# Routed attention and a SoLU layer in one program: cluster products in one pass, u centred in place of w_out, and a new instruction order

## The chip, the core and the metric

The program runs on one core of one Trainium2 chip. The metric is the time of one execution in microseconds (us) of device time. The kernel before takes 224.29 us, the median of three runs (224.18 to 224.49).

The core has five engines, and each works through its own list of instructions in order: TensorE (PE in the profile; its weight loads are PEld), VectorE (DVE), ScalarE (ACT), GpSimd (POOL) and SyncE (SP, which here only issues transfers). They meet at semaphores.

## The reference

```python
q_n = q / (norm(q) + 1e-6)          # k and the centroids c alike
q_assign = argmax(q_n @ c_n.T)      # 16 clusters for each head
k_assign = argmax(k_n @ c_n.T)
mask   = q_assign[:, :, :, None] == k_assign[:, :, None, :]
scores = where(mask, q @ k.T / 8, -1e9)
attn   = softmax(scores)
x      = (attn @ v)                 # 4 batches x 768 tokens, 8 heads x 64 -> 3072 x 512
h      = x @ w_in                   # 512 -> 1024
solu   = h * softmax(h)
ln     = (solu - mean(solu)) / sqrt(var(solu) + 1e-6) * g_ln
out    = ln @ w_out                 # 1024 -> 512
```

There are 4 batches, 8 heads, 768 tokens and a head size of 64. Inputs and output are float32.

## The kernel before, in words

**Attention.** The work goes by batch and by pair of heads: 16 pairs. For each pair q and k are brought to a layout with the head's 64 values on the partitions (`xt`). In the first batch TensorE turns them over; in the other three VectorE does (`xt`, line 444). The pair's products with the centroids (`clusters`, `cl` in the order) are float32 matmuls into `csc`. VectorE then turns `csc` back (`tb`), takes the maximum over the 16 clusters (`mx`), compares (`oh`, the one-hot) and turns the one-hot again (`ot`). The one-hot rows are placed (`pl`) under the bfloat16 copies of q and k (`ca`) in the tile `qk`, so that one matmul of 80 or 96 rows gives score plus bias, and a pair of tokens of different clusters gets a score that the exponential sends to nothing. `bl` blanks the rows that the second head of a pair must not see. Scores (`S`, 294 banks of up to 512 columns) are exponentiated on ScalarE (`E`, line 635), multiplied with v and a column of ones (`V`, 192 blocks of 128 tokens, line 654), and divided by the sums on VectorE (`N`, lines 666 and 679) into `x`.

In the first batch tokens lie so that the pairs 1 to 3 have two tokens in each column of the turned tile (`twelve` in the code is true for them). Their cluster products run in two passes that add up in PSUM, one for each head of the pair, with weights (`c_by_two`) that are zero outside that head's rows: 8 matmuls of 384 columns for a pair (line 484), where a later pair has 4 (line 489).

**The layer.** The 3072 tokens go in 24 blocks f of 128. For each: x is turned (`tx`, a transposing transfer, or TensorE for the first and last), h is made (`h`, 4 parts of two matmuls of 512 columns, line 744), its maximum taken (`hm`, line 750), exponentiated (`ex`, line 756), multiplied (`u` = e * h, line 763), u is turned (`tu`, a transposing transfer, line 768; TensorE and a copy for the last two blocks, lines 732 to 740), the output product runs (`y`, 4 parts, line 813), and the result is scaled by `alpha` (`sc`, lines 830 and 832) and stored (`ou`). The statistics of u (`bn`, `ag`, lines 774 and 778) give `alpha` on GpSimd (`at`, `al`, lines 784 to 793).

The mean of u over the 1024 features must be taken away. The kernel before does it in the weights: with w_g = w_out times g_ln, the mean of w_g over its 1024 rows is taken from each row, and then u needs no centring. That is `su` (8 instructions on VectorE, lines 595 and 598), `me` (TensorE, line 604) and `ce` (8 instructions on VectorE, line 607), once for the program.

**What sets the order.** A class `Weave` holds for each engine a text such as `S2 tp S2 cl S3`: kinds of work in the order in which they stand, where the next of that kind is taken. A second table (`AWAY`) says which pieces run on another engine than their usual one. In a planning pass at build time the class walks through the texts and emits the instructions. The costs given to `add` are used for this plan alone. On the chip an engine does what stands next in its list as soon as what it needs is there, and nothing behind it passes it.

`UNITS`, `BANKS` and `FIRST` (line 279) set in which order the scores of the first batch come: pair 1 with its first and second third of queries, then pairs 2 and 3 alike, and the last thirds of all at the end.

## Time and profile before

| | |
|---|---|
| median of 3 runs | 224.29 us (224.18 to 224.49) |
| span of the profiled execution, first to last instruction | 222.4 us |
| median less span | 1.9 us |
| mean granted TensorE clock | 0.999 |
| matmul work on TensorE, share of the span | 214.8 us, 97% |
| VectorE | 199.1 us, 90% |
| ScalarE | 194.7 us, 88% |
| GpSimd | 126.6 us, 57% |
| first score matmul | 9.90 us |
| first h matmul in the chain of waits | 45.30 us |
| first y matmul | 56.73 us |
| last y matmul ends | 219.03 us |

The page of the profile gives busy time by engine, the chain of waits that ended last (followed back from the last instruction: each step is either work or what it waited for), the costliest groups of instructions with a mean duration, and the transfers. A busy time is the union of an engine's instructions. Matmuls overlap one another in the pipeline, so a busy TensorE can still be standing behind a wait; the chain of waits shows better where it stood.

### The profile page before, as it was taken

How to read it: one execution, taken by the hardware profiler on the slowest of the kernel's cores; microseconds unless marked ns; L12 is line 12 of the kernel's file. 1: busy time of each engine (PE TensorE's matmuls, PEld its weight loads, DVE VectorE, ACT ScalarE, POOL GpSimd, SP SyncE). 2: the span in 40 equal slices, each digit the busy share in tenths (PEclk: the TensorE clock that was granted, in tenths of full speed). 3: DMA queues.
4: the chain of work that ended last, by engine and by line, in shares of the span. 5: the costliest groups of instructions: out<-in, count | busy, mean ns of one | idle time of the engine just before them, and what ended most of it. 6: DMA issues, size and time to landing. Idle time of an engine off the chain costs nothing.

```text
span 222.4 us, 6852 instructions
## 1 busy us (share of the span) xinstructions
PE 214.8 (97%) x2518; PEld 151.8 (68%) x2548; DVE 199.1 (90%) x363; ACT 194.7 (88%) x382; POOL 126.6 (57%) x252
## 2 busy tenths in 40 slices
PE   8999899999999999999999999999999999999993
PEld 7765577767777687777777666676767767665452
DVE  2789999999999999899989999999999979999891
ACT  3899999999999999999999989999999989795352
POOL 3189597759884986188837674783746101226131
PEclk9999999999999999999999999999999999999999
DMA  6998989797799979899999897998922928565623
GB/s 157 352 388 221 193 165 284 203 172 165 127 175 237 180 141 215 136 193 166 153 211 239 156 185 150 151 168 158 230 99 50 115 78 145 117 165 121 166 98 143
DMA packets 122433, 38.74 MB, mean 174 GB/s; under 512 B 111448, under 2 KB 117152, under 8 KB 122400
## 3 DMA queue, kind: packets, MB, share of 16 engines
q1 hardware_dynamic: 121680, 37.82, 79.8%
q10 hardware_dynamic: 720, 0.49, 0.7%
q8 instruction: 20, 0.33, 0.7%
q14 instruction: 13, 0.11, 0.1%
HBM read 23.11 MB, written 6.29 MB: 132 GB/s over the span
## 4 chain that ended last, share of the span: by engine, by line
PE 91%; DVE 3%; issue 2%; ACT 2%; DVEq 0%; ACTq 0%
PE sps L627 27%; PE hreg L744 18%; PE yps L813 17%; PE ops L654 16%; PE csc L489 4%; PE hreg L627 2%; PE idle_p L859 2%; PE csc L484 1%; PE hreg L403 1%; PE hreg L396 1%; ACT qk L468 1%; PE hreg L813 1%; ACT e L635 1%; DVE u L763 1%; DVE w_sum L598 1%
## 5 line engine op out<-in xcount | busy, mean ns | idle before, releaser
L635 ACT ACTIVATE e<-sps 128x512 bf16<-128x512 f32 (+1 forms) x276 | 143.2, 609 | 10.2 <-PE sps L627 9.8
L627 PE MATMUL sps<-qk 96*128 96x256 bf16 (+5 forms) x600 | 87.4, 263 | 0.7 <-ACT e L635 0.4
L627 PEld LDWEIGHTS <-qk 96*128 96x128 bf16 (+1 forms) x636 | 59.6, 121 | 24.5 <-issue 8.8
L654 PEld LDWEIGHTS <-e 128*128 128x128 bf16 x1152 | 49.9, 97 | 9.3 <-issue 1.9
L654 PE MATMUL ops<-v,e 128*128 128x65 bf16 x1152 | 54.3, 193 | 0.4 <-DVE x L679 0.4
L744 PE MATMUL hreg<-w_in_sb,xT 128*128 128x512 bf16 x177 | 48.3, 378 | 0.8
L813 PE MATMUL yps<-w_out_c,uT 128*128 128x512 bf16 x169 | 45.1, 379 | 0.8
L540 POOL COPY qk<-oht 32x384 f32<-32x384 f32 (+1 forms) x49 | 24.2, 494 | 21.5 <-DVE oht L521 15.7
L763 DVE TENSOR_TENSOR u<-e_sb,hreg 128x1024 bf16<-128x1024 bf16 (+1 forms) x25 | 29.1, 1169 | 2.7 <-ACT e_sb L756 2.1
L774 DVE BATCH_NORM_STATS2 bs<-u 128x6 f32<-128x512 bf16 x48 | 31.3, 677 | 0.0
L750 DVE TENSOR_REDUCE nmax<-hreg 128x1 f32<-128x1024 f32 x24 | 29.1, 1213 | 2.0 <-PE hreg L744 1.7
L756 ACT ACTIVATE e_sb<-hreg,nmax 128x1024 bf16<-128x1024 f32 x24 | 26.9, 1121 | 4.5 <-DVE nmax L750 4.4
L790 POOL TENSOR_SCALAR esq<-es,mv 128x1 f32<-128x1 f32 x24 | 8.3, 344 | 33.6 <-DVE mv L778 30.3
L813 PEld LDWEIGHTS <-uT 128*128 128x128 bf16 x200 | 18.0, 97 | 13.1 <-issue 0.3
L744 PEld LDWEIGHTS <-xT 128*128 128x128 bf16 x192 | 17.6, 97 | 11.3 <-ACT e L635 0.3
L472 POOL TENSOR_SCALAR qk<-xt 64x768 bf16<-64x768 f32 (+1 forms) x27 | 22.2, 823 | 3.5 <-DVE xt L444 1.7
L444 DVE STREAM_TRANSPOSE xt<-raw 128x768 f32<-128x768 f32 x24 | 22.2, 949 | 0.0
L470 POOL CAST qk<-xt 64x768 bf16<-64x768 f32 (+1 forms) x25 | 20.9, 836 | 1.2
L679 DVE TENSOR_TENSOR x<-ops,den 128x256 bf16<-128x256 f32 (+1 forms) x39 | 18.9, 486 | 1.3
L784 POOL TENSOR_SCALAR es<-esum 128x1 f32<-128x1 f32 x24 | 5.6, 236 | 20.9 <-ACT e_sb L756 20.4
L793 POOL TENSOR_TENSOR alpha<-esq,halves 128x1 f32<-128x1 f32 x24 | 13.8, 574 | 2.0
L830 ACT ACTIVATE y<-yps,alpha 128x512 f32<-128x512 f32 x15 | 10.4, 695 | 4.3 <-PE yps L813 3.0
(85 smaller groups left out, 206.9 us busy)
## 6 DMA issues: line engine op xcount, KB each, us to landing
vf<-in_v_dram SPq DMA_DIRECT2D x16, 384.0 KB, 4.6
out_dram<-y SPq DMA_DIRECT2D x23, 256.0 KB, 2.5
raw<-in_q_dram SPq DMA_DIRECT2D x50, 96.0 KB, 3.8
raw<-in_k_dram SPq DMA_DIRECT2D x50, 96.0 KB, 3.0
w_g<-in_moe_w_out_dram SPq DMA_DIRECT2D x4, 512.0 KB, 8.3
w_st<-in_moe_w_in_dram SPq DMA_DIRECT2D x4, 512.0 KB, 6.2
raw<-in_q_dram SPq DMA_DIRECT2D x3, 384.0 KB, 6.0
raw<-in_k_dram SPq DMA_DIRECT2D x3, 384.0 KB, 7.8
```

The lines of the kernel that those rows point to most:

```text
L444: nc.vector.transpose(xt[:], raws[b, p, i][:].rearrange("p j c -> p (j c)"))
L472: VEC[e].tensor_scalar(dst, src, scalar1=inv_C, scalar2=1.0, op0=Alu.mult, op1=Alu.mult)
L540: ins = VEC[e].tensor_copy(dst.bitcast(F32), src.bitcast(F32).unsqueeze(1) .to_broadcast([NB, 2, n // 2]))
L627: ins = nc.tensor.matmul(sps_[n, k][:, c0:c0 + w], side(b, h // 2, 1, h % 2, keys)[r], side(b, h // 2, 0, h % 2, slice(s0 * P, s0 * P + w) ...
L635: ins = nc.scalar.activation(es[n, k][:, :w], sps_[n, k][:, :w], Act.Exp, scale=exp_scale, bias=-exp_scale)
L654: nc.tensor.matmul(opss[g][:, s, :VW], es[n, k][:, c0:c0 + P], v1[slot(b, h // 2)][:, h % 2, kt, :VW], start=(kt == 0), stop=(kt == n_t - 1))
L744: uses(nc.tensor.matmul(hreg[:, at(f, f2)[1], :], xTs[f][:, dc, :], w_in_sb[:, dc, f2 * FF2:(f2 + 1) * FF2], start=(dc == 0), stop=(dc == ...
L750: uses(nc.vector.tensor_reduce(ff[f, "nmax"][:], pair_of(f), axis=AXY, op=Alu.max, negate=True), *both(f))
L756: uses(nc.scalar.activation(ff[f, "e"][:], pair_of(f), Act.Exp, bias=ff[f, "nmax"][:], accum_out=ff[f, "esum"][:]), *both(f))
L763: uses(nc.vector.tensor_tensor(ff[f, "u"][:, r], ff[f, "e"][:, r], pair_of(f)[:, r], op=Alu.mult), *both(f)[r])
L774: nc.vector.bn_stats(ff[f, "bs"][:, f2, :], ff[f, "u"][:, f2, :])
L813: ins = nc.tensor.matmul(dst, ff[f, "uT"][:, at(f, f2)[0] * (n_fc // 2) + c, :], w_out_c[:, fc, cols], start=(fc == fcs[0] and turn == 0 i ...
```

## The change

1. For pairs 1 to 3 of the first batch the weights are laid out by token parity instead of by head (`c_two`), so that the products of both heads come in one pass: 4 matmuls in place of 8. The one-hot is then written apart (16 of each 32 columns, tile `apart`), and its turning covers 768 columns in place of 384 (`turned_apart`). A placement copies 16 rows into the one head that it is for, and no blanking is needed for these pairs; the scores of both heads use 80 rows.
2. `su`, `me` and `ce` are gone. `w_out_c` is w_out times g_ln (`gw`, 8 instructions on GpSimd or VectorE). The multiplication that makes u also sums it (`su` as a tile), and a new step `cu` makes u into 1024 u minus its sum, in place: for blocks 0 to 22 one instruction of 1024 columns on GpSimd (13 of them) or on VectorE (10), for the last block two halves on VectorE. The turning and the statistics read the centred u, and the constant under `alpha` is scaled to fit.
3. The first batch takes the first thirds of queries of the pairs 1 to 3 first, then the second thirds, then the last.
4. All five order texts and the table of moved pieces are new, and so are some planning costs. 19 placements are transfers issued by SyncE, where it was 5.

```diff
-    FIRST = [(p, s) for p in range(1, n_pair) for s in range(2)] + [(p, 2) for p in range(1, n_pair)]
+    FIRST = [(p, s) for s in range(3) for p in range(1, n_pair)]
...
-    def clusters(b, p, hf, hh=None):
+    def clusters(b, p, hf):
         lo, n = (0, HALF) if hf is None else (hf * HALF, QTR)
-        if not hh:
-            asg[b, p, hf, "csc"] = ps_m.tile([P, HALF], F32, name="csc", tag="m")
-        csc = asg[b, p, hf, "csc"]
-        if twelve(b, p):
-            for c in range(4):
-                i, part = divmod(c, 2)
-                nc.tensor.matmul(csc[c * NB:(c + 1) * NB, :], c_by_two[:, p, 2 * part + hh, :],
-                                 by_two(b, p, i)[:, hh].rearrange("p t n -> p (t n)"),
-                                 start=(hh == 0), stop=(hh == 1), tile_position=(0, c * NB))
-        for c in range(4) if not twelve(b, p) else ():
+        csc = asg[b, p, hf, "csc"] = ps_m.tile([P, HALF], F32, name="csc", tag="m")
+        for c in range(4):
             i, part = divmod(c, 2)
-            nc.tensor.matmul(csc[c * NB:(c + 1) * NB, :n], c_bd[:, p, :],
-                             xts[b, p, i][:, lo + part * n:lo + (part + 1) * n],
-                             tile_position=(0, c * NB))
+            if twelve(b, p):
+                w = c_two[:, p, part, :]
+                x = by_two(b, p, i)[:, part].rearrange("p t n -> p (t n)")
+            else:
+                w, x = c_bd[:, p, :], xts[b, p, i][:, lo + part * n:lo + (part + 1) * n]
+            nc.tensor.matmul(csc[c * NB:(c + 1) * NB, :n], w, x, tile_position=(0, c * NB))
...
     def assign_turn(b, p, hf):
         n = asg[b, p, hf, "n"]
+        if twelve(b, p):
+            asg[b, p, hf, "oht"] = turned_apart[:, p % 2, :]
+            nc.vector.transpose(turned_apart[:, p % 2, :], apart)
+            return
...
-    def sum_w_out(fc):
...
-    def mean_w_out(x):
...
-    def centre_w_out(fc):
...
+    def scale_w_out(fc, e):
+        VEC[e].tensor_scalar(w_out_c[:, fc, :], w_g[:, fc, :], scalar1=g_ln2[:, fc:fc + 1],
+                             scalar2=None, op0=Alu.mult)
...
-        uses(nc.vector.tensor_tensor(ff[f, "u"][:, r], ff[f, "e"][:, r], pair_of(f)[:, r],
-                                     op=Alu.mult), *both(f)[r])
+        was = ff[f, "su"][:] if half else 0.0
+        ff[f, "su"] = sm.tile([P, 1], F32, name="su", bufs=6)
+        uses(nc.vector.tensor_tensor_reduce(
+            out=ff[f, "u"][:, r], in0=ff[f, "e"][:, r], in1=pair_of(f)[:, r], scale=1.0, scalar=was,
+            op0=Alu.mult, op1=Alu.add, accum_out=ff[f, "su"][:]), *both(f)[r])
+
+    def f_centre(f, e, half=None):
+        u = ff[f, "u"][:] if half is None else ff[f, "u"][:, half]
+        VEC[e].tensor_scalar(u, u, scalar1=float(d_ff), scalar2=ff[f, "su"][:], op0=Alu.mult,
+                             op1=Alu.subtract)
...
-        nc.gpsimd.tensor_scalar(ff[f, "es1"][:], ff[f, "esum"][:], scalar1=1e-3, scalar2=None,
+        nc.gpsimd.tensor_scalar(ff[f, "es1"][:], ff[f, "esum"][:], scalar1=1e-3 * d_ff, scalar2=None,
...
+            add(f"cu{f}", "POOL", 1.1, s + 1, (lambda e, f=f: f_centre(f, e)), made[:1],
+                also={"DVE": 0.36})
...
     ORDER["SP"] = """
-        ld4 si ld3 lv lg ld3 lo lv lo ld2 lo2 lv ld6 lv ld8 li4 tx ld3 lv ld tx lv tu ld10 tx tu ld4
+        ld4 si ld3 lv ld2 lg lv ld2 li lv ld2 lv ld13 li ld li2 lo tx lo2 tx lo pl2 lv tu ld4 pl ld4
```

In the program before and in the one that is changed, the instructions stand as follows at three places. The tile `csc` holds a pair's cluster products, `sps` scores, `ops` the products with v, `hreg` the region of PSUM for h, `qk` the operands of the scores (a number behind it is the buffer), `e` exponentials, `xt` turned q or k, `den` and `x` the reciprocal of the sums and the attention's result, `cst`, `mx`, `oh` and `oht` the steps of the cluster assignment, `nmax` minus the maximum of h, `bs` and `mv` the statistics, `y` and `w_in_sb` the output on its way out (the second name is memory used again). Line numbers of the changed program differ by a few.

The first is TensorE at the first pair with two tokens in a column. Before:

```order
L627 MATMUL sps<-qk_99 128x384
L627 LDWEIGHTS qk_99
L627 MATMUL sps<-qk_99 128x384
L484 MATMUL csc<-xt,w_out_c 32x384 x8
L627 LDWEIGHTS qk_99
L627 MATMUL sps<-qk_99 128x384
```

The change:

```order
L407 MATMUL hreg<-ident_f,raw 128x128 x9
L622 LDWEIGHTS qk_99
L622 MATMUL sps<-qk_99 128x384
L622 LDWEIGHTS qk_99
L622 MATMUL sps<-qk_99 128x384
L622 LDWEIGHTS qk_99
L622 MATMUL sps<-qk_99 128x384
L490 MATMUL csc<-xt,w_out_c 32x384 x4
```

The eight products became four, and they stand after the third score bank, where they stood after the ninth.

The second is VectorE from the cluster assignment of that pair to the first division by the sums. Before:

```order
L515 TENSOR_TENSOR oh<-cst,mx 128x384
L521 STREAM_TRANSPOSE oht<-oh 128x384
L470 CAST qk_100<-xt 64x6x128
L472 TENSOR_SCALAR qk_101<-xt 64x6x128
L430 COPY xt<-hreg 128x384
L588 COPY g_ln_115<-gps 128x8
L595 TENSOR_SCALAR w_sum<-w_g,g_ln_115 128x512
L598 SCALAR_TENSOR_TENSOR w_sum<-w_g,g_ln_115,w_sum 128x512
L666 RECIPROCAL den<-ops 128x6
```

The change:

```order
L522 TENSOR_TENSOR w_out_c<-cst,mx 128x12x2x16
L434 COPY xt<-hreg 128x384
L597 COPY g_ln_115<-gps 128x8
L528 STREAM_TRANSPOSE w_out_c<-w_out_c 128x768
L476 TENSOR_SCALAR qk_100<-xt 64x6x128
L474 CAST qk_101<-xt 64x6x128
L661 RECIPROCAL den<-ops 128x6
```

The two sums over w_out ahead of the division are gone, and the turning of the one-hot is twice as wide.

The third is SyncE around the loads of w_out (`w_g`); in the program before the four stand between the 14th and the 18th row, ahead of nearly all loads of the later batches. The change:

```order
L583 DMA w_st<-in_moe_w_in_dram 128x1024 x2
L600 DMA w_g<-in_moe_w_out_dram 128x2x512
L704 DMA_TRANSPOSE xT<-x 128x4x128
L600 DMA w_g<-in_moe_w_out_dram 128x2x512 x2
L704 DMA_TRANSPOSE xT<-x 128x8x128
L600 DMA w_g<-in_moe_w_out_dram 128x2x512
L549 DMA qk_103<-oht 32x2x384 x2
```

The last quarter of w_out now stands behind the transposing transfer of x for the blocks 2 and 3.

243 lines of the change are left out of this document (117 added, 126 removed).

## Prediction

> **What bounds the kernel now.** I read the page's busy times first, then a table of busy time by stretch, then the chain of waits from its end to its beginning, and last the groups of instructions.
>
> ```profile
> PE 214.8 (97%) x2518; PEld 151.8 (68%) x2548; DVE 199.1 (90%) x363; ACT 194.7 (88%) x382; POOL 126.6 (57%) x252
> ```
>
> Three engines lie between 88 and 97%, so the next question is who waits for whom, by stretch (columns: stretch, its length, then busy time and instruction count of PE, PEld, DVE, ACT and POOL):
>
> ```profile
> 10.00:45.00 35.00, 33.88 (x445) 24.11 (x445) 32.79 (x65) 34.48 (x77) 27.25 (x49) 1.00 0.91 246
> 45.00:170.00 125.00, 123.45 (x1422) 89.19 (x1440) 118.11 (x205) 118.72 (x230) 84.14 (x153) 1.00 0.89 169
> 170.00:200.00 30.00, 29.62 (x370) 20.93 (x376) 27.47 (x46) 27.12 (x52) 5.28 (x14) 1.00 0.64 122
> ```
>
> Up to 45 us there is no work of the layer yet, only attention: ScalarE is full (34.48 of 35.00), and VectorE nearly. From 45 to 200 us the layer's matmuls fill TensorE's gaps, and TensorE is full. The granted clock is 1.00 throughout, so it is no term. In the chain of waits (start, length, engine, tile and line), TensorE hands over to VectorE once for long in the first part:
>
> ```profile
> 19.01 0.09 DVE xt L430
> ...
> 19.68 0.82 DVE w_sum L595
> ...
> 20.52 1.19 DVE w_sum L598
> ...
> 23.40 0.56 DVE xt L430
> ...
> 24.09 0.60 PE hreg L627 x4
> ...
> 26.36 1.43 PE csc L484 x16
> ...
> 33.66 0.57 PE ops L654 x18
> 34.23 0.22 PE sps L627 x2
> 34.45 0.78 PE csc L489 x8
> ...
> 37.78 0.43 PE hreg L604 x2
> ...
> 40.10 0.51 PE hreg L604 x2
> ```
>
> From 19.01 to 24.09 the path is VectorE's list: the two first sums over w_out stand ahead of the first division, whose result frees the PSUM tile for the next products. So the time is TensorE's list, plus the places where it stands: that one, the start, and the end.
>
> **The change part by part.** The sum is made against the profiled execution: a span of 222.4 us, which is 1.9 us under the median of 224.29 us; I add these 1.9 us at the end.
>
> *TensorE's own work.* A pair's two-pass cluster products take 1.43 us in the chain, a one-pass pair of 384 columns takes 0.78. Three pairs go from the one to the other: 3 x 0.65 = 1.95 us. The two mean products (0.43 and 0.51) go: 0.94 us. Nothing is added on TensorE; turning, scores and layer keep their counts. As TensorE is the path behind 45 us, and both pieces lie ahead of it in one list, I count all: **-2.9 us**. The bounds: -1.9 if the cluster products that lay beside the VectorE path (one of the three, 0.65) and some of the rest were covered anyway, -2.9 otherwise.
>
> *VectorE.* Its groups (count | total, mean ns of one | idle before):
>
> ```profile
> L763 DVE TENSOR_TENSOR u<-e_sb,hreg 128x1024 bf16<-128x1024 bf16 x23 | 27.9, 1213 | 2.7 <-ACT e_sb L756 2.1
> L444 DVE STREAM_TRANSPOSE xt<-raw 128x768 f32<-128x768 f32 x24 | 22.2, 949 | 0.0
> ...
> L521 DVE STREAM_TRANSPOSE oht<-oh 128x384 bf16<-128x384 bf16 x15 | 8.5, 565 | 0.1
> L515 DVE TENSOR_TENSOR oh<-cst,mx 128x384 bf16<-128x384 f32 x15 | 8.4, 563 | 0.1
> ...
> L598 DVE SCALAR_TENSOR_TENSOR w_sum<-w_g,g_ln,w_sum 128x512 f32<-128x512 f32 x7 | 5.9, 837 | 0.1
> L607 DVE SCALAR_TENSOR_TENSOR w_out_c<-w_g,g_ln,hreg 128x512 bf16<-128x512 f32 x8 | 5.5, 740 | 0.0
> ...
> L558 DVE CAST v<-vf 128x384 bf16<-128x384 f32 x7 | 2.4, 357 | 0.0
> L470 DVE CAST qk<-xt 64x768 bf16<-64x768 f32 x4 | 2.3, 586 | 0.1
> ...
> L515 DVE TENSOR_TENSOR oh<-cst,mx 128x192 bf16<-128x192 f32 x2 | 0.7, 357 | 0.1
> ...
> L887 DVE CUSTOM_DVE_ANT_0 c_n<-c_all 128x64 f32<-128x64 f32 x1 | 0.2, 226 | 1.5 <-DMA c_all<-in_centroids_dram 1.5
> ...
> L887 DVE DVE_READ_ACCUMULATOR2_ANT c_nsq<- 128x1 f32 x1 | 0.1, 83 | 0.0
> ```
>
> Gone: 0.8 + 7 x 0.84 = 6.7 us of sums and 5.5 us of centring w_out, 12.2 us, all ahead of 47 us. Added once: three one-hot turns of 768 columns in place of 384, 3 x (0.95 - 0.57) = 1.2 us. The rest of VectorE's pieces is exchanged with ScalarE and GpSimd nearly evenly (two casts of q or k and two of v more, three uT copies, two scalings and three blanks fewer), which I take as zero.
>
> Added for each block: the product that makes u becomes the fused product and sum. The trace has that instruction once, at 64 columns: 226 ns, and 83 ns for reading the sum out. Two-input instructions of 192 and 384 columns take 357 and 563 ns, which is 1.07 ns a column and 151 ns fixed; at 64 columns that line gives 220 ns. So the fused form runs at the plain rate at 64 columns, and I take 1.21 us at 1024, as before, plus 0.08 us: 24 x 0.08 = 2 us. The lower end is 0 more; the upper, if nothing of the 226 ns were fixed, would be 3.5 ns a column and 3.6 us each. The lines of 192 and 384 columns are nearer, so I stay with the plain rate.
>
> The ten centrings on VectorE and the two halves: the trace has no bfloat16 to bfloat16 instruction with SBUF on both sides. Casts from float32 take 357 ns at 384 columns and 586 at 768: 0.6 ns a column, hence 0.74 us at 1024. Half the bytes on the input could halve it, 0.37; running at the two-input rate it would be 1.25. I take 0.55, and 0.33 for a half: 10 x 0.55 + 0.66 = 6.2 us (4.2 to 13). Together VectorE changes by -12.2 + 1.2 + 2 + 6.2 = -2.8 us (-4.8 to +4), but ahead of 47 us it loses some 11 us and behind it gains some 8. There it was busy 118.1 + 27.5 = 145.6 of 155 us: the 9.4 us of idle time cover it, barely.
>
> [...]
>
> *The stand at 19 us.* VectorE has 2.0 us of sums less ahead of the first division, and the wider turn (0.4) and another cast (0.6) more; the new list is some 1 us shorter there. **-1.0 us** (0 to -2).
>
> *ScalarE.* It is full up to 45 us, and in the chain its casts of q and k stand right ahead of its first exponential:
>
> ```profile
> 10.18 0.52 ACT qk L468
> 10.70 0.38 ACT e L635
> ```
>
> It loses four such half casts, 2.1 us, and a full one. Most lay ahead of that first exponential, where the first scores are the other condition, so only a part shows: I count **-0.5 us** (0 to -2).
>
> *The start.* The chain and the list at the first assignment:
>
> ```profile
> 7.38 0.38 DVE L497 STREAM_TRANSPOSE cst<-csc 128x192 f32<-128x192 f32 x1 [1.13 <-PE csc L489]
> ```
>
> In the new list the copies of the second half of q and k, a cast and the wider weights stand ahead of this turn, and TensorE's cluster products for the first half wait behind its transposes of the second. The idle 1.13 us ahead of it takes some of them. I take the first scores **+0.6 us** later (0 to +1.2).
>
> *The first output product.* It needs all of w_out, and the last quarter is now loaded behind the transfer that turns x for the blocks 2 and 3, which itself waits for the eighth division.
>
> ```profile
> 43.85 0.18 DVE L666 RECIPROCAL den<-ops 128x4 f32<-128x4 f32 x1
> ...
> 45.03 3.03 SPq L709 DMA_TRANSPOSE xT<-x  x1
> ```
>
> ```profile
> w_g<-in_moe_w_out_dram SPq DMA_DIRECT2D x4, 512.0 KB, 8.3
> w_st<-in_moe_w_in_dram SPq DMA_DIRECT2D x4, 512.0 KB, 6.2
> ```
>
> ```profile
> L578 POOL CAST w_in_sb<-w_st 128x512 bf16<-128x512 f32 x8 | 4.7, 614 | 2.5 <-DMA w_st<-in_moe_w_in_dram 2.4
> ```
>
> ```profile
> 56.73 1.24 PE yps L813 x5
> ```
>
> Ahead of the first y the new list has 4 score banks (0.22 each) and 3 blocks of v (0.57) less, besides the 2.9 us: 4.3 us, so TensorE comes to it at about 56.7 - 4.3 - 1.5 + 0.6 = 51.5 us. The eighth division comes near 42.5; the transfer behind it takes its 1.2 to 3 us of issue, the load 6 to 8 us, and two scalings of some 0.7 us on GpSimd (the 614 ns cast plus a scalar) follow: 50.5 to 55 us. I take a wait of **+0.7 us** (0 to +3.5).
>
> *The centring on the way.* On GpSimd it costs about 1.05 us a block (two of the 614 ns casts, less one fixed part), 13 us in all, on an engine with 95 us idle. It lengthens the way from h to y: hm 1.2, ex 1.3, u 1.2, centring 1.05, the turning transfer 3.4 (the row of uT<-u below), some 8.2 us. Between the last h of a block and its first y the new list has at least 10.8 us of other work on TensorE for blocks 1 to 20, and 8.6 for block 0, whose centring is on VectorE. So it costs nothing while that holds; without it each block could cost up to 1 us.
>
> ```profile
> uT<-u SPq DMA_TRANSPOSE x22, 3.4
> qk<-oht SPq DMA_DIRECT2D x5, 48.0 KB, 2.0
> ```
>
> *The end.* For the last block both halves of u must be summed before either is centred, so its first turn comes about 1.4 us later; two more y parts stand ahead of it on TensorE (0.86 us), and the chain there had 2 us to spare. The last two scalings stood on two engines and are now both on VectorE:
>
> ```profile
> 218.79 0.53 ACT L830 ACTIVATE w_in_sb<-hreg,alpha 128x320 f32<-128x320 f32 x1 [0.87 <-PE hreg L813]
> 219.13 0.42 DVE L832 TENSOR_SCALAR w_in_sb<-hreg,alpha 128x192 f32<-128x192 f32 x1 [1.40 <-PE hreg L813]
> ```
>
> The second then starts 0.2 us later: **+0.3 us** (0 to +0.8).
>
> Sum: -2.9 - 1.0 - 0.5 + 0.6 + 0.7 + 0.3 = -2.8 us; 222.4 - 2.8 = 219.6, and with the 1.9 us around the span **221.5 us**.
>
> **The rivals.**
>
> *VectorE or new waits behind 45 us eat the gain.* For it: 9.4 us of idle time against some 8 us more work, and three engines near full; a centring at 0.74 us makes it 10. Against: TensorE's list has other work between. It would give back about 2 us: 223.6 us.
>
> *w_out comes late.* With a load of 8.3 us behind a transfer of 3 us the first y starts at 55 us, 3.5 us behind TensorE's list, and the sum is 0: 224.3 us. For it: the rows above; against: the four loads of 6.2 us were issued in a bunch, a single one may be quicker.
>
> *SyncE's queue.* 19 placements instead of 5 (2.0 us to landing, against 0.5 us on GpSimd) each wait for a one-hot with q, k and v loads behind them. If that delays two or three pairs by 1.5 us each: 226 us. Against: loads are issued long ahead.
>
> *Slower: the fused product.* At half the plain rate u takes 2.3 us, 1.1 us more in each of 24 blocks: 26 us on an engine with 9.4 us idle and 2.8 us gained. It then sets the pace, and the time is about 222.4 - 2.8 + 26 - 9.4 + 1.9 = 238 us. It decides from about 0.5 us more for each block. The 64-column row speaks against it. [...]
>
> **How the numbers follow.** Forecast 0.58, with its own range 219.6 to 223.2; VectorE or new waits 0.18; w_out late 0.10; SyncE's queue 0.08; the slow fused product 0.06. A measurement of this kernel tells about 0.2% (0.45 us) from no change. Faster takes nearly all of the forecast, two thirds of the next and little of the third: 0.71; no change 0.11; slower 0.18. The range, 218.6 to 225.2, takes in the forecast's bounds, the second and third case, and leaves out the slow fused product, most of SyncE's case and the best ends of all terms together.
>
> **What would show it.** Right: 8 TensorE records of 0.78 us for each of the three pairs, no VectorE path at 19 us, first y ahead of 55 us, u near 1.25 us with a read-out behind it. Wrong: a wait of the first y on the w_out scaling or its load; waits of h on u, or of y on the turning, between 60 and 200 us; u above 1.7 us; first scores after 11.2 us.

## The result and the profile after

The change takes 248.7 us (median of four runs, 247.2 to 250.5) against 224.2 for the kernel before (223.7 to 224.5): a ratio of 1.110, with a 95% interval of 1.104 to 1.116. The prediction said 221.5 us and faster; it was wrong in sign and by 27 us. The profiled execution has a span of 247.1 us, 24.7 more than before. Times and ratios of the experiments leave out executions in a slower state with a lower clock, so that a time can lie up to 1 us under the one that a later expectation names.

The page of the changed kernel, busy times first, then the chain that ended last by engine and by line:

```profile
PE 223.7 (91%) x2520; PEld 153.8 (62%) x2520; DVE 202.5 (82%) x389; ACT 196.5 (80%) x380; POOL 176.4 (71%) x248
...
PE 37%; POOL 32%; DVE 10%; DMA 8%; issue 6%; SPq 5%; ACT 1%; POOLq 0%; DVEq 0%; ACTq 0%
POOL u L767 15%; PE sps L622 11%; PE ops L649 7%; PE yps L817 6%; PE hreg L739 6%; DMA raw<-in_q_dram 5%; POOL qk L474 3%; SPq L440 3%; PE csc L490 3%; DVE bs L778 2%; POOL qk L476 2%; POOL alpha L797 2%; DVE u L760 2%; POOL w_out_c L603 2%; PE hreg L407 2%
```

The same line of the kernel before:

```profile
PE 91%; DVE 3%; issue 2%; ACT 2%; DVEq 0%; ACTq 0%
```

TensorE was 91% of the chain and is 37% now. GpSimd, which had no part in it, is 32%, and almost half of that is one line: the centring of u (L767). The groups of instructions say why (count | total, mean ns of one | idle before):

```profile
L767 POOL TENSOR_SCALAR u<-u,su 128x1024 bf16<-128x1024 bf16 x13 | 48.6, 3736 | 11.3 <-DVE su L760 7.2 <-issue 2.5 <-DVE den L661 0.6
L760 DVE CUSTOM_DVE_ANT_0 u<-e_sb,hreg 128x1024 bf16<-128x1024 bf16 x23 | 27.8, 1208 | 2.9 <-ACT e_sb L751 2.9
L603 POOL TENSOR_SCALAR w_out_c<-w_g,g_ln 128x512 bf16<-128x512 f32 x7 | 11.1, 1583 | 0.3
L767 DVE TENSOR_SCALAR u<-u,su 128x1024 bf16<-128x1024 bf16 x10 | 5.4, 536 | 0.1
L528 DVE STREAM_TRANSPOSE w_out_c<-w_out_c 128x768 bf16<-128x768 bf16 x3 | 2.9, 973 | 0.1
L490 PE MATMUL csc<-xt,w_out_c 128*32 128x384 f32 x24 | 2.6, 498 | 0.0
L760 DVE DVE_READ_ACCUMULATOR2_ANT su<- 128x1 f32 x25 | 2.1, 83 | 0.0
```

A centring takes 3.74 us on GpSimd and 0.54 on VectorE. The forecast had 1.05 and 0.55. A scaling of w_out takes 1.58 us, where it had 0.7. The fused product (1.21 us, 83 ns to read the sum out), the wide turn (0.97 us) and the cluster products (four for each pair, 24 records in all, as each leaves two) came out as costed. GpSimd's instructions stand in the trace in the order of its list, so what stands behind a centring waits too: the statistics of the 11th block (L782) start at 166.11 us and take 0.17, and the step on GpSimd that takes them (L794) starts at 170.18, right behind a centring of 3.73. The waits (engine and line, for whom, us in total, times, longest) and the same stretches as before:

```profile
ACT e L630 <- PE sps L622: 19.9, 30, 2.3
...
DVE bs L778 <- POOL u L767: 9.7, 8, 2.6
...
PEld L622 <- POOL qk L560: 5.6, 2, 3.1
...
ACT y L834 <- POOL alpha L797: 3.7, 5, 1.1
```

```profile
10.00:45.00 35.00, 32.51 (x373) 22.21 (x366) 28.75 (x56) 30.00 (x67) 22.79 (x39) 0.85 0.86 210
45.00:170.00 125.00, 114.02 (x1293) 80.06 (x1290) 106.62 (x196) 109.52 (x209) 96.91 (x125) 1.00 0.85 170
170.00:200.00 30.00, 26.11 (x296) 18.35 (x294) 24.86 (x44) 23.72 (x46) 23.42 (x34) 0.94 0.42 93
```

No engine is full any more in any stretch: TensorE is busy 114.0 of 125 us where it was 123.5, ScalarE 109.5 where it was 118.7. They wait for each other across GpSimd.

The granted clock, 0.85 in the first row, has a share of this execution:

```profile
30.00:35.00 5.00, 4.56 (x45) 3.60 (x43) 3.31 (x7) 4.26 (x9) 4.29 (x9) 0.50 1.01 349
35.00:40.00 5.00, 5.00 (x46) 2.81 (x44) 2.20 (x7) 2.56 (x6) 1.64 (x3) 0.57 0.22 81
```

The 51st exponential of the scores starts 4.4 us later than in the kernel before. In the run below in which only the form of the centring differs (240.4 us), it is 1.6 us, with the clock at 1.00 in these stretches. So some 3 us of the profiled execution go with the clock, an estimate from these two; the one with the highest clock (0.993) took 247.2 us, still 23 us more than before.

In the chain around the first output product:

```profile
57.52 0.49 DVE oht L531
58.05 1.55 POOL w_out_c L603
59.60 0.20 POOL es L788
59.80 3.08 POOL w_out_c L603 x2
```

### The profile page after: what moved, and what is told of

Same layout as the page of the kernel before. It is cut to its first block, busy times and chain, and to the rows that moved or that the text cites. A ratio compares the mean times of both kernels' runs of the same rounds, so it can differ in the third digit from the quotient of the medians.

```text
span 247.1 us, 6865 instructions
## 1 busy us (share of the span) xinstructions
PE 223.7 (91%) x2520; PEld 153.8 (62%) x2520; DVE 202.5 (82%) x389; ACT 196.5 (80%) x380; POOL 176.4 (71%) x248
## 4 chain that ended last, share of the span: by engine, by line
PE 37%; POOL 32%; DVE 10%; DMA 8%; issue 6%; SPq 5%; ACT 1%; POOLq 0%; DVEq 0%; ACTq 0%
POOL u L767 15%; PE sps L622 11%; PE ops L649 7%; PE yps L817 6%; PE hreg L739 6%; DMA raw<-in_q_dram 5%; POOL qk L474 3%; SPq L440 3%; PE csc L490 3%; DVE bs L778 2%; POOL qk L476 2%; POOL alpha L797 2%; DVE u L760 2%; POOL w_out_c L603 2%; PE hreg L407 2%
## 5 line engine op out<-in xcount | busy, mean ns | idle before, releaser
L630 ACT ACTIVATE e<-sps 128x512 bf16<-128x512 f32 (+1 forms) x280 | 145.5, 600 | 21.3 <-PE sps L622 19.9
L622 PE MATMUL sps<-qk 80*128 80x256 bf16 (+5 forms) x608 | 94.8, 268 | 9.2 <-POOL qk L560 4.9
L622 PEld LDWEIGHTS <-qk 80*128 80x128 bf16 (+1 forms) x636 | 62.1, 123 | 40.1 <-issue 8.9
L649 PEld LDWEIGHTS <-e 128*128 128x128 bf16 x1152 | 54.2, 100 | 17.8 <-DVE x L674 3.6
L649 PE MATMUL ops<-v,e 128*128 128x65 bf16 x1152 | 59.4, 197 | 4.7 <-DVE x L674 2.5
L767 POOL TENSOR_SCALAR u<-u,su 128x1024 bf16<-128x1024 bf16 x13 | 48.6, 3736 | 11.3 <-DVE su L760 7.2
L739 PE MATMUL hreg<-w_in_sb,xT 128*128 128x512 bf16 x192 | 54.9, 382 | 1.3 <-DMA xT<-x 0.8
L817 PE MATMUL yps<-w_out_c,uT 128*128 128x512 bf16 x184 | 50.7, 382 | 0.9 <-ACT y L834 0.6
L778 DVE BATCH_NORM_STATS2 bs<-u 128x6 f32<-128x512 bf16 x48 | 32.1, 681 | 9.8 <-POOL u L767 9.7
L760 DVE CUSTOM_DVE_ANT_0 u<-e_sb,hreg 128x1024 bf16<-128x1024 bf16 (+1 forms) x24 | 28.5, 1186 | 3.0 <-ACT e_sb L751 2.9
L551 POOL COPY qk<-oht 32x384 f32<-32x384 f32 (+1 forms) x32 | 16.3, 510 | 15.4 <-DVE oht L531 13.8
L794 POOL TENSOR_SCALAR esq<-es,mv 128x1 f32<-128x1 f32 x24 | 8.3, 347 | 16.8 <-DVE mv L782 15.8
```

The lines of the kernel that those rows point to most:

```text
L622: ins = nc.tensor.matmul(sps_[n, k][:, c0:c0 + w], side(b, h // 2, 1, h % 2, keys)[r], side(b, h // 2, 0, h % 2, slice(s0 * P, s0 * P + w) ...
L630: ins = nc.scalar.activation(es[n, k][:, :w], sps_[n, k][:, :w], Act.Exp, scale=exp_scale, bias=-exp_scale)
L649: nc.tensor.matmul(opss[g][:, s, :VW], es[n, k][:, c0:c0 + P], v1[slot(b, h // 2)][:, h % 2, kt, :VW], start=(kt == 0), stop=(kt == n_t - 1))
L739: uses(nc.tensor.matmul(hreg[:, at(f, f2)[1], :], xTs[f][:, dc, :], w_in_sb[:, dc, f2 * FF2:(f2 + 1) * FF2], start=(dc == 0), stop=(dc == ...
L760: uses(nc.vector.tensor_tensor_reduce(out=ff[f, "u"][:, r], in0=ff[f, "e"][:, r], in1=pair_of(f)[:, r], scale=1.0, scalar=was, op0=Alu.mul ...
L767: VEC[e].tensor_scalar(u, u, scalar1=float(d_ff), scalar2=ff[f, "su"][:], op0=Alu.mult, op1=Alu.subtract)
```

## The experiments

All ratios are to the kernel before on the same chip, with 95% intervals.

**Is it the operand?** The first theory was that an operand that differs by row makes the instruction slow on GpSimd. Two runs put a constant in its place, first in the centring, then in the scaling as well:

```
-  scalar1=float(d_ff), scalar2=ff[f, "su"][:]       # on GpSimd
+  scalar1=float(d_ff), scalar2=0.5
```

> The change with the centring on GpSimd subtracting a constant where it subtracted the row's own sum from a tile (13 blocks; the centring is then wrong there, the instruction's size, place and order are the same). Theory A (an operand that differs by row makes the instruction slow on GpSimd): one centring falls from 3.73 us to 0.9 to 1.2 us, GpSimd's busy time by some 34 us from 176, and the kernel from 248.7 to 224 to 230 us, the rest being the scalings of w_out (1.58 us each), the late start and the new order. Rival B (128 x 1024 bfloat16 in place is slow on GpSimd whatever the operand): it stays at 3.7 us and 248 us. Rival C (the new order, the placements on SyncE or a lower granted clock cost the time, the slow centring lies beside it): a short centring, but still over 238 us.

> As the run before, and the seven scalings of w_out on GpSimd multiply by a constant where they multiplied by g_ln of the row (the factor g_ln is left out there). Theory A: one scaling falls from 1.58 us to 0.6 to 0.75 us, the first output product from 66.6 us to about 58 to 61 us, and the kernel to 221.5 to 226 us: what is left over the forecast of 221.5 us is the start (+1.3 us above what was forecast) and waits of the new order. Rival B: scalings stay at 1.58 us, no gain on the run before. Rival C: over 235 us.

Measured: 245.7 us (1.097, 1.090 to 1.104) and 244.3 us (1.091, 1.084 to 1.098); a centring 3.67 us, a scaling 1.50. The theory fell: the operand is worth 2% of a centring and 6% of a scaling. Rival B, slow whatever the operand, stood so far.

**Away from GpSimd.**

```
-  POOL: ... pl4 cu bl ...        DVE: ... u bn2 N ...
+  POOL: ... pl4 bl ...           DVE: ... u cu bn2 N ...      # all 13
```

> The change with all centrings on VectorE, each right behind the fused product of its block; GpSimd's list is otherwise the same, the result is the reference's. VectorE gets 13 x 0.54 = 7.0 us more, GpSimd loses 48.6 us. Theory A or B: 223 to 229 us, with the scalings of w_out still at 1.58 us on GpSimd and the first output product near 66 us. Rival C: over 238 us. If VectorE, 202.5 us busy in the run of the change, becomes the bound, waits of the layer's hidden products on the fused product show, and the time is above 229 us.

Measured: 234.7 us (1.048, 1.038 to 1.057). Some 14 us of the loss hang on the centring's place on GpSimd. But it stays 11 us above the kernel before, over the range that theories A and B gave.

**Which form is slow?** Two kernels with other operations in the place of the centrings:

> Prices. The change with other operations in the place of the thirteen centrings on GpSimd (blocks 4 and 5 as they are; 7 and 8 one operation with the row's sum as operand; 9 and 11 two operations with constants; 13 and 14 one with a constant; 16 and 18 a tensor_tensor with the sum spread along the row; 19 and 20 a tensor_tensor with a second full tile, e; 21 a plain copy); the centring is left out or changed in 11 blocks. Theory A: 3.7 us for the first two, 3.0 to 3.7 for the next two, 0.9 to 1.2 for constants and for the copy, 1.1 to 1.6 for tensor_tensor. Rival B: 3 us or more for all of them.

> Prices, since it is the arithmetic on GpSimd that is slow, with either kind of operand: 3.65 us for two operations with constants, 2.79 for one, 1.04 for a plain copy; yet the two-operation scaling of q and k (multiply, multiply; 64 x 768) takes 0.86. The change with other forms in the place of the centrings on GpSimd (blocks 4 and 5 multiply, multiply; 7 and 8 multiply, subtract on 64 rows; 9 and 11 multiply, multiply on 64 rows; 13 and 14 multiply, add; 16 and 18 multiply by the row's sum, then by 1.0; 19 and 20 not in place, into the tile of e; 21 on 512 columns); the centring is left out or changed in all 13. Theory A2 (the pair of operations decides, multiply-multiply is a fast form): blocks 4, 5, 9 and 11 1.0 to 1.3 us, the others 3.6, 512 columns 1.9. Theory B2 (64 rows are cheaper): blocks 7 to 11 near 1.1 to 1.9, all on 128 rows 3.6. Theory C2 (in place is slow): 19 and 20 near 1.1, all others 3.6.

Groups of GpSimd in the first of them: two operations with the row's sum (L770), two with constants (L774), one with the sum (L772), one with a constant (L776), a tensor_tensor with a full tile (L780), with the sum spread along the row (L778), a copy (L782):

```profile
L770 POOL TENSOR_SCALAR u<-u,su 128x1024 bf16<-128x1024 bf16 x2 | 7.4, 3724 | 0.4 <-POOL qk L476 0.3
L774 POOL TENSOR_SCALAR u<-u 128x1024 bf16<-128x1024 bf16 x2 | 7.3, 3649 | 0.2
...
L772 POOL TENSOR_SCALAR u<-u,su 128x1024 bf16<-128x1024 bf16 x2 | 5.7, 2854 | 3.1 <-issue 3.0
L776 POOL TENSOR_SCALAR u<-u 128x1024 bf16<-128x1024 bf16 x2 | 5.6, 2788 | 0.1
L780 POOL TENSOR_TENSOR u<-u,e_sb 128x1024 bf16<-128x1024 bf16 x2 | 4.2, 2124 | 3.9 <-DVE su L760 3.9
L778 POOL TENSOR_TENSOR u<-u,su 128x1024 bf16<-128x1024 bf16 x2 | 3.8, 1894 | 6.5 <-DVE su L760 6.5
...
L782 POOL COPY u<-u 128x1024 bf16<-128x1024 bf16 x1 | 1.0, 1036 | 1.1 <-DVE su L760 1.1
```

In the second: multiply, subtract into another tile (L782) and on 64 rows (L774); multiply by the row's sum, then by 1.0 (L780); multiply, multiply with constants (L772); multiply, add (L778); multiply, multiply on 64 rows (L776):

```profile
L782 POOL TENSOR_SCALAR e_sb<-u 128x1024 bf16<-128x1024 bf16 x2 | 7.3, 3652 | 3.2 <-DVE su L760 3.0
L774 POOL TENSOR_SCALAR u<-u 64x1024 bf16<-64x1024 bf16 x2 | 7.3, 3637 | 2.3 <-DVE su L760 2.2
...
L780 POOL TENSOR_SCALAR u<-u,su 128x1024 bf16<-128x1024 bf16 x2 | 2.2, 1116 | 5.1 <-DVE su L760 5.1
L772 POOL TENSOR_SCALAR u<-u 128x1024 bf16<-128x1024 bf16 x2 | 2.1, 1044 | 0.2
L778 POOL TENSOR_SCALAR u<-u 128x1024 bf16<-128x1024 bf16 x2 | 2.1, 1040 | 0.1
L776 POOL TENSOR_SCALAR u<-u 64x1024 bf16<-64x1024 bf16 x2 | 2.1, 1040 | 0.1
```

So theory A2 holds, and wider than it was put: multiply-multiply and multiply-add run at the rate of a copy (1.04 us), with constants and, for multiply-multiply, with an operand per row (1.12). Multiply-subtract takes 3.65 and a single operation 2.8 us. Neither rows nor place matter (64 rows: 3.64 and 1.04 us; into another tile: 3.65). A single operation was tried as a multiplication and as a subtraction. The whole kernels took 239.8 and 235.3 us, in one execution each.

**The same mathematics in the fast form.** The fused product takes its negative, so that the sum is negative and can be added; the scaling gets a second multiplication by 1.0:

```
-  in1=pair_of(f)[:, r], scale=1.0,            op0=mult, op1=subtract, scalar1=d_ff
+  in1=pair_of(f)[:, r], scale=-1.0,           op0=mult, op1=add,      scalar1=-d_ff
-  scalar1=g_ln2[:, fc:fc + 1], scalar2=None, op0=mult
+  scalar1=g_ln2[:, fc:fc + 1], scalar2=1.0,  op0=mult, op1=mult
```

> The change with both GpSimd operations written in the form that ran at the rate of a copy: the centring as multiply, add (the fused product takes its negative, u and its sum come out negative, times -1024, plus the negative sum), the scaling of w_out as multiply by g_ln, then multiply by 1.0. Same order, same results, same engines. Theory E (the form of the two instructions is what made the loss): centring 1.04 to 1.12 us in place of 3.73, scaling 0.6 to 0.7 in place of 1.58, GpSimd busy 135 us, kernel 219.5 to 224 us; nearly all of the 24.5 us comes back. Rival D (VectorE, with 8 us more behind 45 us, and the order's waits for w_out and at the start cost several us of their own): 226 to 232 us.

> As f1, but the scaling of w_out left in its slow form (one multiplication, 1.58 us): tells the centring's share from the scaling's. The first output product waited on the scaling from 58 to 66 us in the run of the change. Theory E with a share for w_out: 1.5 to 4 us above f1; if VectorE's list takes the wait up: within 0.5 us.

Measured, both: 231.7 us (1.034, 1.030 to 1.037); the centring alone in the fast form: 240.4 us (1.075, 1.072 to 1.077). The groups with both:

```profile
L767 POOL TENSOR_SCALAR u<-u,su 128x1024 bf16<-128x1024 bf16 x13 | 14.7, 1131 | 17.7 <-DVE su L760 11.4 <-issue 3.0 <-DVE den L661 2.0
L603 POOL TENSOR_SCALAR w_out_c<-w_g,g_ln 128x512 bf16<-128x512 f32 x7 | 5.0, 714 | 0.3
```

The two forms make some 17 of the 24.5 us. The kernel whose scalings stay slow is 8.7 us above the one with both fast, where 1.5 to 4 us were expected. Only 3.8 us of this arise where the scalings stand: the 91st exponential starts at 66.3 against 62.5 us, the 73rd at the same time within 0.1 us. Another 5 us come near 128 us, where a turning transfer of u takes 5.73 us in that profile (3.90 in the other) and TensorE is busy 5.89 of the 10 us from 130 to 140 us, at a mean clock of 0.66. Why the transfer takes longer there was not tried. Between theory E and rival D the answer is both: the forms are the larger part, and 8 us are something else.

**The order's own places.** Two runs mended the places that the chain showed, one with the centring on VectorE, one with the fast forms:

```
-  SP:   li2 lo tx lo2 tx lo          POOL: wi4 pl gw2 ca gw     PE: cl tp2 fl2 cl
+  SP:   li2 lo4 tx2                  POOL: wi4 gw7 pl ca        PE: cl fl2 cl tp2
   (in the first of the two gw4 on POOL and four gw on DVE)
```

> The centring all on VectorE as in the run before of that kind (235.5 us), and three places of the order mended: the four loads of w_out on SyncE ahead of the two transfers that turn x (they waited 7.3 us behind one), four scalings of w_out on GpSimd ahead of the placement for which it stood idle 8.0 us and four on VectorE, and the second half's cluster products of the first pair ahead of the transposes of the next pair. Theory A3 (the order's own waits make up what is left): first output product from 63.8 us to 54 to 57 us, first scores from 11.6 us to 10.2 to 10.8, the kernel 230 to 232 us. Rival D (VectorE's list is the bound behind 45 us, whatever comes earlier is waited for there): 234 to 236 us.

> As f1, and the three mends of the order: the four loads of w_out on SyncE ahead of the two transfers that turn x, the seven scalings on GpSimd ahead of the placement they stood behind, the second half's cluster products of the first pair ahead of the transposes of the next pair. If the late start and the late w_out still cost in f1: 1 to 3 us less than f1, that is 217.5 to 222 us; if the list of VectorE or ScalarE takes them up: within 0.5 us of f1.

Measured: 232.3 us (1.040, 1.034 to 1.046; without the mends 1.048, and the intervals overlap), and 234.2 us (1.047, 1.042 to 1.052), which is slower than without them. The first score came at 11.5 and 12.1 us, against 9.9 before and 11.5 to 11.6 without the mend. So the order of those products is not what holds the start. Only the early w_out may have helped, and not where the scaling is fast anyway.

**SyncE's placements.** All placements of the later batches on GpSimd, in the fast-form kernel:

```
-  SP:   19 pl (batches 1 to 3)
+  POOL: 19 more pl, behind the first pl of the same pair
```

> f1 (the change with the fast forms, 232.2 us) with the fourteen placements and five more that stood on SyncE now on GpSimd, right behind the first placement of their pair there. Theory S (SyncE's queue: a placement that waits for its one-hot holds the v loads and turning transfers behind it; in f1 the chain has a 3.9 us turning at 122 us and a 4.7 us load of v at 135 us, and TensorE falls 5 us behind its list at block 10 and gets 3 of them back): 227.5 to 230.5 us and a smaller spread. Rival V (VectorE's list, without idle time from 5 to 70 us, sets the pace, the placements don't): 231 to 233 us; GpSimd's extra 19 x 0.5 us could even make it slower.

Measured: 230.4 us (1.031, 1.028 to 1.034) against 231.7 (1.034, 1.030 to 1.037). The medians differ by 1.2 us, the ratios by 0.5 us, and the intervals overlap: at most a small share, not shown.

**Are the parts worth anything in the old order?** First the clusters alone, then both parts with the centring on VectorE:

```
   before.py's order
+  c_two / apart / turned_apart, one pass of four products;  - 3 blanks
   and, in the second: + u centred on VectorE, + gw where ce stood, - su, - me
```

> The kernel before, in its own order, with the one-pass cluster products and the wider one-hot turn alone (the three blanks, which this form doesn't need, are gone). By the prediction's terms: TensorE -1.95 us, of which one pair (0.65) may lie beside VectorE's list; VectorE three wider turns, +1.2 us ahead of 40 us: 222 to 223.5 us against 224.1. Rival (the cluster products lie beside waits on ScalarE and VectorE, full up to 45 us): 223.7 to 225 us.

> Both parts of the change in the order of the kernel before: one-pass cluster products, u centred (all 24 blocks on VectorE, right behind the fused product), w_out scaled on VectorE where it was centred, no sums over w_out, no mean products. Theory A3 (GpSimd's price and the new order make the loss, the parts do not): TensorE -2.9 us, VectorE -12.2 + 1.2 + 2.0 + 24 x 0.54 = +4 us in all but -11 ahead of 45 us: 221.5 to 225 us. Rival D (behind 45 us VectorE gets 15 us more with 9.4 us idle): 226 to 232 us.

Measured: 224.6 us (1.0045, 1.0020 to 1.0071) and 232.1 us (1.038, 1.033 to 1.043). The clusters alone are no gain, slightly a loss, and the second run came out at the upper end of rival D's range, without any of the new order and without any centring on GpSimd. The chain of the first, where the cluster assignments stand:

```profile
13.06 0.83 PE csc L486 x8
...
13.91 0.59 DVE cst L492
...
14.53 0.56 DVE mx L505
...
15.11 1.10 DVE w_out_c L518
...
16.24 0.98 DVE w_out_c L524
```

The time that TensorE no longer needs here (0.83 in place of 1.43 us) goes to the wider one-hot and turn on VectorE (1.10 and 0.98 us, where the kernel before has 0.56 and 0.58). Behind them the chain stays on VectorE, over casts and a copy, until the sums over w_out.

**The centring taken away.** The same kernel without the centring, in the old order and, with the fast forms otherwise, in the new one:

```
-  VEC[e].tensor_scalar(u, u, scalar1=..., scalar2=ff[f, "su"][:], ...)
+  pass
```

> Both parts in the order of the kernel before (232.1 us) without the centring: u goes uncentred to the products (the mean is left out), all else is the same, so VectorE loses 24 instructions of 0.5 to 0.6 us. Rival D confirmed (VectorE's extra work behind 45 us is what those 8 us are): 222 to 224.5 us. If it stays above 228 us, the fused product or another part takes them.

> f1 (the change, fast forms, 232.2 us) without the centring on either engine (the mean is left out): 13 instructions of 1.1 us less on GpSimd and 10 of 0.6 and two halves less on VectorE, in the new order. In the old order leaving the centring out gave 8.3 us (232.1 to 223.8). If the centring is what still costs: 223 to 226 us. If the new order itself costs (VectorE's first 70 us, v loads and turnings at block 10): 228 to 231 us.

Measured: 223.8 us (0.999, 0.997 to 1.001) and 232.5 us (1.036, 1.030 to 1.042). In the old order the centring is the whole loss, 8.3 us for the 14.6 us that these groups of the kernel with it take on VectorE, and all that the change removes is worth nothing clear of the noise even so:

```profile
L766 DVE TENSOR_SCALAR u<-u,su 128x1024 bf16<-128x1024 bf16 x23 | 14.0, 610 | 0.8
...
L766 DVE TENSOR_SCALAR u<-u,su 128x512 bf16<-128x512 bf16 x2 | 0.6, 352 | 0.0
```

In the new order taking it away gains nothing: there the 8 us are not the centring. They come with the order texts, the table of moved pieces and what else differs between the two kernels. One such thing is not in the list of changes: only 14 score banks of the first batch go through the region of PSUM for h, where 18 did (`spare_to` 58 in place of 66). It was not tried alone.

The same stretch (columns as in the prediction), first of the kernel before, then of the old-order kernel without centring:

```profile
9.00:43.00 34.00, 32.88 (x425) 22.88 (x419) 31.75 (x64) 33.46 (x75) 26.23 (x48) 1.00 0.93 258
```

```profile
9.00:43.00 34.00, 32.24 (x408) 21.80 (x405) 29.07 (x58) 33.93 (x76) 24.68 (x46) 1.00 0.94 259
```

VectorE is relieved by 2.7 us. ScalarE, which had 0.54 us of idle time in these 34, has 0.07 left: it takes what there is and is the bound. From the first exponential of the scores to the 61st, in the same two kernels:

```profile
10.61:42.07 31.46, 30.34 (x402) 21.67 (x400) 29.34 (x59) 30.95 (x70) 24.65 (x43) 1.00 0.91 254
```

```profile
10.66:41.14 30.48, 29.32 (x374) 20.10 (x372) 25.71 (x49) 30.45 (x70) 22.59 (x41) 1.00 0.95 263
```

So a lead of 0.9 us is there at 41 us. By the 73rd exponential 0.4 us of it are left (49.61 against 49.97 us), and 0.2 to 0.4 us stay to the end of the scores. In between VectorE's eight scalings of w_out stand, 0.47 to 1.60 us each and 6.4 us in all, where the kernel before has eight instructions of 5.5 us, and one of them is in the chain of waits. That they take the lead back was not tried. The profiled execution is the slowest of ten (222.4 to 224.2 us); the three fastest lie near 222.8, below all 17 of the kernel before beside them.

**ScalarE, tested.**

> Both parts in the old order without the centring (223.8 us; the mean is left out), and seven pieces of the first batch moved from ScalarE to VectorE, which has 2 of 10 us idle there: five copies of transposed q and k (0.4 us each) and two casts (0.8). In that run ScalarE has no idle time from 8.7 to 43 us, its exponentials of the first batch stand back to back. Theory A4 (the 2.9 us saved on TensorE and the 12 us of VectorE don't show because ScalarE sets the time up to 43 us): 3.6 us of relief, 220.5 to 222.8 us. Rival (TensorE's list, 9.6 of 10 us busy there, is as long): 223.3 to 224.3 us.

> As x1 (no sums over w_out, no mean products, no centring: the mean is left out; old order, 223.8 us), with the two-pass cluster products of the kernel before: three pairs of 1.43 us on TensorE in place of 0.78, all ahead of 35 us. In x1 ScalarE is busy 33.93 of the 34.00 us from 9 to 43 us. Theory A4 (ScalarE sets the time there, so 1.95 us less on TensorE are worth nothing): 223.3 to 224.3 us, the same as x1. Rival (TensorE's list counts): 225.2 to 226 us.

The first (seven names moved from ScalarE's table of places to VectorE's) took 227.2 us (1.015, 1.011 to 1.019), a miss that tells nothing on the question: three of the moved copies and a cast now stand in VectorE's list ahead of the weights of the later clusters and of a cast of v, on which TensorE then waits. From 10 to 20 us TensorE was busy only 7.72 us and ScalarE 5.45. The second (the two-pass products put back) took 224.0 us (1.002, 0.999 to 1.005) against 223.8 with one pass. So 1.95 us of TensorE's work ahead of 35 us are worth 0.3 us by the medians and 0.6 by the ratios, and the intervals overlap. The two-pass form also brings back the narrower one-hot and turn, which take some 0.7 us less for each pair on VectorE, so this run does not tell TensorE's share from VectorE's. ScalarE as the bound up to 42 us agrees with both busy times and this run. That relief of ScalarE would bring the gain out was not shown.

**Is there a better version?** Two tries started from the old order, 22 of 24 centrings on GpSimd in the fast form, with and without the one-pass clusters:

> Both parts with the fast forms, starting from the order of the kernel before: 22 of 24 centrings on GpSimd, five of eight scalings of w_out there, and instructions of VectorE and GpSimd moved by a few places so that statistics and other work stand between a fused product and what needs the centred u. If the parts were worth something once GpSimd's price is right and VectorE's list is spared: 220 to 223.5 us, faster than before's 223.9. If the cost is VectorE's first 70 us: 224 to 227 us.

> As h1 without the one-pass cluster products: only u centred in place of w_out, 22 centrings and three scalings on GpSimd. The cluster part alone measured +0.5 us, so it is worth nothing there: the same as h1 within 1 us, 220 to 224 us, if the gain is that of the sums and mean products that are gone; 1 to 2 us above h1 if the one-pass products pay once VectorE has no sums ahead of 45 us.

Measured: 231.6 us (1.036, 1.033 to 1.039) and 228.5 us (1.022, 1.019 to 1.024), both slower. In both, scalings of w_out stand ahead of the last cluster assignments of the first batch, whose one-hots (in the second kernel the weights) lie in the same tile, so those are overwritten and that part of the computation is spoiled. The work issued is the same; that no duration hangs on the data was not tried. As the old-order kernel without any centring only equals the kernel before, none of these versions was followed further. No version beat the kernel before.

## Why the prediction was wrong, step by step

**The step that failed first** is "On GpSimd it costs about 1.05 us a block (two of the 614 ns casts, less one fixed part)". It is 3.74 us. The price was that of a cast, and nothing bounded it from above: VectorE's centring got two ends, GpSimd's got none. The claim behind it, "it costs nothing while that holds", fell with it, as did "two scalings of some 0.7 us" (1.58). What the runs showed in its place: a multiplication and a subtraction in one instruction of GpSimd take 3.5 times as long as a copy of the same size, and what stands behind them in GpSimd's list waits; the two forms together cost some 17 us. With the fast form the same steps take 1.13 and 0.71 us, so the two estimates were right for a form that the change doesn't use. In the runs of forms a copy, multiply-multiply and multiply-add take 1.04 us for 1024 columns (1.0 ns a column), one operation alone 2.8 and multiply-subtract 3.65.

**"TensorE's own work, -2.9 us ... I count all"** had the right sizes (some 0.8 us a pair; the mean products gone) and no effect clear of the noise. In the old order, both parts without the centring bring 0.1%. The bound to apply stood in the row I had quoted: ScalarE busy 34.48 of 35.00 us up to 45 us. What other engines save there could bring no more than about ScalarE's idle half microsecond, and the cluster products, the sums and most of the stand lie there. The traces of that kernel and the kernel before show a lead of 0.9 us at 41 us, and 0.4 us at 50; what took the rest is open. The **stand at 19 us** (-1.0) fell in the same way. **ScalarE's casts** (-0.5) can't be read off these runs: in the change the scores start later and ScalarE is busy 30.0 of 35 us.

**VectorE's sum** (-2.8 us, -4.8 to +4) came out at +3.4: busy 202.5 against 199.1 us, near its upper bound. The terms that were priced came out as priced (12.2 us gone; the wider turns 1.2, reading the sums out 2.1, the centrings 6.0). What it took as zero, the exchange of the other pieces, is the rest, some 6 us: more placements, casts of w_in and a scaling of w_out on VectorE, the wider one-hot, and longer pieces, as casts of v (464 ns, 357 before) and of q and k (714, 586 before). The reasoning from it failed too: "the 9.4 us of idle time cover it, barely". They didn't cover it. In the old order 14.6 us of centring cost 8.3, which is the first rival's mechanism at four times its price. Busy time and the longer way from h to y were not told apart there.

**The start** (+0.6) was +1.7: first score at 11.6 us, outside the bound of 11.2 that was given as a sign. The mend tried for it did not help, so its cause stays open.

**The rivals.** The slow fused product fell: no run shows the half rate that it took (2.3 us), the fused product takes 1.21. SyncE's queue is not told apart from zero. The late w_out was real: the first y stood behind the scaling, one of the signs given, but through the scaling's form. None of them was "an instruction moved to GpSimd is slow there", which is the mechanism that decided; the chances summed to one without it.

**What stays open** are some 8 us that the new order costs with the fast forms. TensorE stands 3.8 us between 9 and 43 us (1.1 before), and VectorE is busy 31.4 us there, as much as before (31.75) with the sums gone; casts in its list take up to 1.01 us where one of the same size takes 0.56 (below). Yet most of the loss arises later. Counting the exponentials of the scores, whose order differs a little, the fast-form kernel is 1.9 us late at the 61st (43.96 us against 42.07), 1.0 at the 121st (near 81 us) and 5.5 at the 161st (108.63 us against 103.11). Without the centring it is 0.7 us late, then 0.7 ahead, then 9.3 late. In the fast-form kernel the chain runs from 94.8 to 108.3 us over VectorE, GpSimd and one step of ScalarE, without TensorE:

```profile
101.97 0.90 POOL alpha L797
102.86 0.79 POOL qk L474
```

In the kernel without centring GpSimd stands there for a load of v, and VectorE stands ahead of a turning of q or k for what the profile doesn't show (88 to 112 us, columns as for the waits above):

```profile
POOL v L569 <- DMA vf<-in_v_dram: 6.3, 1, 6.3
...
DVE xt L448 <- issue: 3.0, 1, 3.0
```

Near block 10 a turning and a load of v are long again. From the fast-form kernel's chain:

```profile
122.21 3.90 DMA uT<-u
...
134.71 4.65 DMA vf<-in_v_dram
```

The exponentials don't fall further behind there, from 5.7 us at the 181st (121.8 us) to 4.9 at the 211th. The placements on SyncE (L549) stand ahead of such loads, but without them the time is the same within the intervals. Which part of the order makes the loss was not found.

## What to carry to other kernels

Price an instruction from a row of the same engine and the same operations; where there is none, measure it alone first. A bound from the slowest row of that engine would not have been enough here: the kernel before's slowest copy on GpSimd (662 ns for 384 columns, L533) gives 1.8 us for 1024 columns, an estimate at half of what the centring took. Cap the gain of a stretch by the idle time of its fullest engine, not of the one whose work is removed. And measure the parts of a change in the old order too: there these parts showed as no gain within a run or two.

## What the runs showed of the hardware

**GpSimd's tensor_scalar has fast and slow forms.** For 1024 columns of bfloat16 on 128 rows: copy 1.04, multiply-multiply and multiply-add 1.04, multiply-multiply with an operand per row 1.12, one operation 2.8, multiply-subtract 3.65, tensor_tensor 1.9 to 2.1 us. A multiplication takes 2.79 us alone (by a constant) and 1.12 with a second one by 1.0 behind it (by the row's sum), 2.5 times less; the scaling of w_out (float32 to bfloat16, 512 columns) goes from 1.58 to 0.71 us. On 64 rows multiply-subtract takes 3.64 and multiply-multiply 1.04 us.

**Some of VectorE's casts took longer while GpSimd worked.** In the fast-form kernel, two casts of q or k of the same size on VectorE, one while GpSimd works and one while it is idle (from 37.9 to 45.1 us), with GpSimd's instruction between:

```profile
21.77 1.01 DVE L474 CAST qk<-xt 64x768 bf16<-64x768 f32 x1
```

```profile
21.55 0.82 POOL L474 CAST qk<-xt 64x768 bf16<-64x768 f32 x1
```

```profile
40.79 0.56 DVE L474 CAST qk<-xt 64x768 bf16<-64x768 f32 x1
```

1.01 against 0.56 us; casts of v in that kernel take 0.32 to 0.98. The long cast starts 0.22 us after GpSimd's and ends 0.41 us after its end. Three copies of VectorE out of PSUM (L434, 384 columns) take 0.54 us, two of them while GpSimd works. Not every cast is longer beside GpSimd: in the profile of the change the casts of this size take 0.74, 1.01, 0.56 and 0.71 us while it works and 0.56 while it is idle (at 43.66 us). No run here changed this alone, so neither the cause nor what it costs the kernel is measured.

**The granted clock was below 1.00 in some stretches**: 0.85 on average from 10 to 45 us in the profile of the change (0.50 and 0.57 from 30 to 40 us), with TensorE busy 32.51 of 35 us, 0.83 from 10 to 20 us in the run with less on ScalarE (busy 7.72 of 10 us), and 0.66 from 130 to 140 us in the run whose scalings stay slow (5.89 of 10 us). It stayed at 1.00 in the fast-form kernel with TensorE busy 30.19 of 34 us between 9 and 43 us. What decides it was not tried.
